# Attention packs and channel mixer on one core: another order of the opening's 939 words

## The chip, the cores and the metric

One core of a Trainium2 chip runs the whole program. The metric is the device time of one execution in microseconds (us); the time before is the median of three runs, 764.49 us (764.2 to 765.55).

## The reference, cut to what matters

```python
def sm_attn(qq, kk, vv):
    s = scale * np.matmul(qq, kk.transpose(0, 1, 3, 2))
    a = np.exp(s - np.max(s, axis=-1, keepdims=True))
    return np.matmul(a / (np.sum(a, axis=-1, keepdims=True) + 1e-09), vv)

# q, k, v: 8 batches, 8 heads, 576 rows, 64 columns; p: 32 packs for each head
p_packed = sm_attn(p, k, v)                # phase 1
out = sm_attn(q, p_packed, p_packed)       # attention of a batch
x = out.transpose(0, 2, 1, 3).reshape(8, 576, 512)
h = x.transpose(0, 2, 1) @ U @ V           # mix along the rows, rank 32
u = x + h.transpose(0, 2, 1)
return u + np.maximum(u @ w_ch1, 0) @ w_ch2    # 512 -> 2048 -> 512
```

U, V, w_ch1 and w_ch2 come as 64-bit floats and are converted on the chip.

## The kernel before, in words

Phase 1 packs the attention of p over k and v for all 8 batches. Its unit is four heads of one batch, so there are 16 units. For each the kernel loads k (`lk`) and v (`lv`, three DMAs), turns k in three pieces on TensorE (PE; `k0`, `k1`, `k2`) and copies each piece out of PSUM into `kT` (`k0a`, `k1a`, `k2a`, lines 310 and 312), multiplies with p (`s0`, line 321), takes the row maximum on VectorE (DVE; `s1`) and the exponential on ScalarE (ACT; `s2`), turns the result back (`b0`, `b1`, lines 327 and 329), copies that into `eT` (`b0a`, `b1a`, lines 672 and 674), and multiplies with v (`m0`, line 696, 40 matmuls: "the unit's product"). `m1` scales the product, `m2` keeps it, `h0` (line 709) turns it, `h1` (line 715) copies it and `h2` stores it for later.

The first batch is worked in between. The weights arrive as 512 KB blocks of bits (`w0` for w_ch1, `z0` for w_ch2) in a ring of two buffers (four for some early ones). A block is converted in a serial chain: one step on ACT (`w1`, `z1`, line 79), three on DVE (`w2` to `w4`, `z2` to `z4`, lines 80 to 82); w_ch2 is then split into a high part on ACT (`z5`, line 214) and a low part on DVE (`z6`, line 218), since matmuls here run as three products of high and low parts. `q0` to `q2` with their copies, `s3` to `sa`, `t0` to `t3`, `x0` to `x2` and `y0` to `y3` are the attention and the row mix of batches 0 and 1. `f0` folds packs into w_ch1 (line 562; `f1`, `f2` split it), `g0` is half a block of the first product of the channel mixer (six matmuls, lines 100 to 102), `e0`, `e1` and `l0` its high part, its last rows and its low part, `G0` a tile of the second product, `ad` the residual.

One string, `opening`, writes the order of all this by hand: 939 words. The program walks through it and calls, for every word, the next stage of that name (`lk` the next unit's k load, and so on). Nothing is reordered after that: each engine, and SP's queue of DMAs, works its own instructions in the order in which the words issue them, and waits where another engine's result or a free buffer is missing. A word that ends in an extra `v` puts a copy on DVE; without it the copy is ACT's. This choice exists for 116 copies: the `k?a`, `b?a` and `q?a` words, `p1` and `h1`. SP's queue holds the loads and stores: `lk`, `lp`, `lv`, `w0`, `z0`, `u0`, `v0`, `a0`, `h2`, `pu`, `ge`.

PSUM tiles come in pairs of banks by tag: `k` for the turns of k and for `g0`; `t` for p0, the heads, the folds and all of the attention; `m` for b0, b1 and m0 until `G0` starts. A word takes a free bank of its pair when it is issued. k has three buffers in SBUF, v three, and one bank pair `s` serves `s0` alone. Behind the opening a loop over the blocks of the second batch begins, and then strings of words for batches 2 to 7; these don't change. Its first step issues two halves of the first product and then the last four tiles (kt = 15) of the first batch's second product, which need the last block of w_ch2.

Of the kernel before, what the change touches and what calls it, by code (L numbers as in the profile page):

```python
# [20 lines left out]
def packed_attention_mixer_kernel(  # L21
# [49 lines left out]
    U, V, w1, w2 = (a.bitcast(I32) for a in (U, V, w1, w2))  # L71
# [83 lines left out]
    def bits_tile():  # L155
        return pipe.tile([P, 512, 2], I32, name="bits", bufs=2)

    opening = (
# [28 lines left out]
    )  # L187
    NW1 = 8

# [1153 lines left out]
    for b in late:  # L1343
        s0, s1 = sweeps[b]
# [94 lines left out]
```

## Time and profile before

| | before |
|---|---|
| median of three runs | 764.49 us |
| the profiled execution | 765.2 us, its span 763.2 |
| PE, PE's weight loads | 749.9 us (98%), 662.2 us (87%) |
| DVE, ACT, POOL | 587.5 (77%), 405.7 (53%), 84.9 us (11%) |
| DMA | 151.78 MB, mean 199 GB/s |
| granted TensorE clock | 1.0 throughout |

The span runs from the first to the last instruction; the execution's own time lies 2.0 us above it. PE's busy time counts each matmul from its start to its modelled end, and these overlap. A window gives, for one stretch, busy time of each engine and the share of the 16 DMA engines. A chain of waits is followed back from the last instruction: each piece was released by the one before it. "Landing" is the time from the issue of a DMA to the arrival of its last byte.

### The profile page before, as it was taken

How to read it: one execution, taken by the hardware profiler on the slowest of the kernel's cores; microseconds unless marked ns; L12 is line 12 of the kernel's file. 1: busy time of each engine (PE TensorE's matmuls, PEld its weight loads, DVE VectorE, ACT ScalarE, POOL GpSimd, SP SyncE). 2: the span in 40 equal slices, each digit the busy share in tenths (PEclk: the TensorE clock that was granted, in tenths of full speed). 3: DMA queues.
4: the chain of work that ended last, by engine and by line, in shares of the span. 5: the costliest groups of instructions: out<-in, count | busy, mean ns of one | idle time of the engine just before them, and what ended most of it. 6: DMA issues, size and time to landing. Idle time of an engine off the chain costs nothing.

```text
span 763.2 us, 19553 instructions
## 1 busy us (share of the span) xinstructions
PE 749.9 (98%) x7795; PEld 662.2 (87%) x7795; DVE 587.5 (77%) x1216; ACT 405.7 (53%) x1018; POOL 84.9 (11%) x116
## 2 busy tenths in 40 slices
PE   8999999999999999999999999999999999999997
PEld 6667787887878889998999989999999989999997
DVE  4799789976787768867888768867887678764876
ACT  4788765554343645555455544555554554555451
POOL 1123111010111002100201002010201020200000
PEclk9999999999999999999999999999999999999999
DMA  9999984369112874656478474657464746463672
GB/s 318 337 355 305 324 219 157 112 228 300 40 42 88 254 250 140 221 195 200 130 229 267 132 245 148 185 168 244 145 192 166 253 126 202 148 239 125 198 224 105
DMA packets 106090, 151.78 MB, mean 199 GB/s; under 512 B 40464, under 2 KB 60176, under 8 KB 102416
## 3 DMA queue, kind: packets, MB, share of 16 engines
q1 hardware_dynamic: 105856, 150.28, 61.6%
q8 instruction: 62, 1.02, 0.5%
q14 instruction: 28, 0.23, 0.1%
q10 hardware_dynamic: 144, 0.26, 0.1%
HBM read 116.56 MB, written 33.95 MB: 197 GB/s over the span
## 4 chain that ended last, share of the span: by engine, by line
PE 85%; DMA 6%; DVE 4%; ACT 3%; issue 1%; SPq 0%; POOL 0%; ACTq 0%
PE o L1085 33%; PE h_ps L100 9%; PE h_ps L101 8%; PE h_ps L102 8%; PE t_ps L562 4%; PE o L100 3%; PE o L101 3%; PE o L102 3%; DMA w1s<-w1D 2%; DMA kx<-in_k_dram 2%; PE t_ps L301 1%; PE o L1114 1%; PE s_ps L321 1%; PE t_ps L321 1%; PE m_ps L696 1%
## 5 line engine op out<-in xcount | busy, mean ns | idle before, releaser
L1085 PE MATMUL o<-w2h,h 128*128 128x256 f32 x832 | 166.9, 281 | 0.0
L100 PE MATMUL h_ps<-ah,wth 128*128 128x256 f32 (+1 forms) x512 | 157.5, 308 | 0.6 <-ACT hj L801 0.3
L101 PE MATMUL h_ps<-al,wth 128*128 128x256 f32 (+1 forms) x512 | 150.4, 294 | 0.0
L102 PE MATMUL h_ps<-ah,wtl 128*128 128x256 f32 (+1 forms) x512 | 150.3, 294 | 0.0
L1085 PEld LDWEIGHTS o<-w2h,h 128*128 128x128 f32 x832 | 136.2, 189 | 2.6 <-issue 2.6
L1074 DVE TENSOR_TENSOR h<-bits,h 128x896 fp32r<-128x896 f32 (+1 forms) x104 | 107.8, 1037 | 31.2 <-ACT h L1069 30.5
L1069 ACT CAST h<-bits 128x896 fp32r<-128x896 f32 (+1 forms) x104 | 93.7, 901 | 58.0 <-DVE bits L1048 39.7
L100 PEld LDWEIGHTS h_ps<-ah,wth 128*128 128x128 f32 x512 | 96.4, 188 | 25.2 <-ACT ppall L1034 8.4
L1085 PE MATMUL o<-w2l,h 128*128 128x256 f32 x416 | 116.0, 279 | 0.0
L101 PEld LDWEIGHTS h_ps<-al,wth 128*128 128x128 f32 x512 | 96.3, 188 | 1.0
L102 PEld LDWEIGHTS h_ps<-ah,wtl 128*128 128x128 f32 x512 | 96.3, 188 | 0.0
L1034 ACT ACTIVATE bits<-h_ps 128x256 f32<-128x256 f32 x132 | 49.5, 385 | 67.4 <-PE h_ps L102 51.5
L1085 PE MATMUL o<-tb,h 128*128 128x256 f32 x468 | 81.2, 282 | 0.1
L1085 PEld LDWEIGHTS o<-w2l,h 128*128 128x128 f32 x416 | 78.1, 188 | 0.0
L576 DVE TENSOR_TENSOR wtl<-t_ps,wth 128x256 fp32r<-128x256 f32 x128 | 49.4, 417 | 29.4 <-ACT wth L574 28.3
L1085 PEld LDWEIGHTS o<-tb,h 128*128 128x128 f32 x468 | 66.7, 189 | 0.6 <-DVE h L1074 0.3
L1046 DVE TENSOR_TENSOR bits<-bits 128x256 f32<-128x256 f32 x96 | 42.9, 447 | 28.6 <-ACT bits L1034 28.4
L574 ACT CAST wth<-t_ps 128x256 fp32r<-128x256 f32 x128 | 42.6, 376 | 27.0 <-PE t_ps L562 20.4
L452 POOL TENSOR_TENSOR al<-aT,ah 128x320 fp32r<-128x320 f32 (+1 forms) x32 | 31.4, 985 | 207.0 <-ACT ah L448 178.4
L100 PE MATMUL o<-w2h,h 128*128 128x512 f32 x128 | 52.1, 407 | 0.0
L101 PE MATMUL o<-w2l,h 128*128 128x512 f32 x128 | 50.6, 395 | 0.0
L102 PE MATMUL o<-w2h,h 128*128 128x512 f32 x128 | 50.5, 395 | 0.0
(212 smaller groups left out, 1379.8 us busy)
## 6 DMA issues: line engine op xcount, KB each, us to landing
w1s<-w1D SPq DMA_DIRECT2D x24, 1024.0 KB, 5.5
tc<-tD SPq DMA_DIRECT2D x94, 256.0 KB, 3.1
bits<-in_moe_w_ch_dram SPq DMA_DIRECT2D x32, 512.0 KB, 4.6
kx<-in_k_dram SPq DMA_DIRECT2D x16, 576.0 KB, 5.9
x<-in_q_dram SPq DMA_DIRECT2D x16, 576.0 KB, 5.9
out_dram<-os SPq DMA_DIRECT2D x33, 256.0 KB, 2.9
vt<-in_v_dram SPq DMA_DIRECT2D x32, 256.0 KB, 6.1
hD<-ppall SPq DMA_DIRECT2D x30, 256.0 KB, 4.1
```

The source lines that it names most:

```text
L100: nc.tensor.matmul(ps, lhsT=lh, rhs=rh, start=start, stop=False)
L101: nc.tensor.matmul(ps, lhsT=lh, rhs=rl, start=False, stop=False)
L102: nc.tensor.matmul(ps, lhsT=ll, rhs=rh, start=False, stop=stop)
L452: nc.gpsimd.tensor_tensor(al, aT[:, ns], ah.bitcast(F32), op=ALU.subtract)
L562: nc.tensor.matmul(f_ps[g][xs], lhsT=ppT[b][zs, g, xs], rhs=w[zs, h // 2], start=True, stop=True)
L574: nc.scalar.copy(hi[:, g], src)
L576: nc.vector.tensor_tensor(lo[:, g], src, hi[:, g].bitcast(F32), op=ALU.subtract)
L1034: nc.scalar.activation(dst[:, 256 * (i % 2):256 * (i % 2) + 256], src, AF.Relu)
L1046: vec(l[:, 4:6], s[:, 1:3], s[:, 0:1].to_broadcast([P, 2, P]), op=ALU.add)
L1069: nc.scalar.copy(h[:, ks], src)
L1074: nc.vector.tensor_tensor(lo[:, ks], src, h[:, ks].bitcast(F32), op=ALU.subtract)
L1085: nc.tensor.matmul(ps, lhsT=a, rhs=b, start=x not in self.begun, stop=last and i == 2)
```

## The change

The 939 words of `opening` stand in another order; each name occurs as often as before. 45 of the 116 copies change engines: 26 go from ACT to DVE (`k0a` five, `b1a` five, `k1a` four, `h1` three, `p1`, `b0a`, `k2a` and `q2a` two each, `q0a` one), 19 from DVE to ACT (`h1` five, `k2a` four, `b0a` four, `k1a`, `p1` and `q1a` two each). ACT has 85 of them before and 78 after. The diff replaces the whole string; its first lines, the place around the last product of phase 1, and its last lines:

```diff
-        "w0 lk lp u0 lk lk lp w1 w2 k1 k2 p0 k1av v0 k2a w0 u1 k0 p1 u2 w3 k0a lk k2 u2 lp u2 s0 k2a w0 u3 lv k0 s1 "
-        "k1 k0a w4 v3 k1a k0 lk s2 k1 k0av k1a s0 u3 b0 s1 p0 b1 k2 p1 k1 s2 k2av lk b0av lp k0 v1 r0 w0 v2 b1 s0 lv "
...
-        "w4 s3 sa w0 e1 e0 ad h2 l0 s4 s4 s5 w1 l0 s6 m0 w2 g0 w3 m1 m2 G0 w4 e0 w1 g0 l0 w0 w2 G0 w3 h0 G0 w4 h1 s7 "
...
-        "e1 z1 z6 G0 z2 G0 z3 G0 e0 f2 g0 z4 l0 G0 e0 f2 f1 l0 G0 z1 z5 g0 z2 z6 G0 z3 g0 e0 f2 y2 z4 G0 y3 e0 e1 l0 "
-        "f1 G0 z5 pu G0 z6 G0 f2 l0 "
+        "lk k1 lp lp p0 p0 lk v0 k0 lk lv p1 k1av k0av k0 w0 k2 k2a lp lk k2 k2a s0 s1 k1 s2 b1 b0 k0a k0 k1av s0 b0a "
+        "k0av lk k1 v1 k2 k1a k2a s1 p0 k0 p1v u0 w0 w0 lp lk k1 k1av s2 s0 w1 b1 k1 w2 v2 v2 b1av b1av k0a s1 k1av lv "
...
+        "h0 lv h1 w2 g0 w3 w1 h0 G0 e0 G0 w4 w0 s8 h1 w2 g0 q1a w3 w4 t0 s3 r1 e0 z6 w1 s9 sa s4 ad s4 s5 m0 s6 s7 w0 "
...
+        "e1 g0 z6 G0 e0 l0 g0 G0 z1 z2 z3 z4 y2 G0 y3 y2 y2 z5 f1 e1 G0 f1 z0 z1 f2 z6 G0 f2 G0 z2 e0 e0 l0 g0 G0 l0 z3 "
+        "G0 g0 z4 e1 z5 z6 y2 G0 G0 G0 e0 z1 z2 e0 l0 l0 z3 z4 y3 z5 z6 f1 f1 f2 f2 y3 y3 G0 "
```

What stands ahead of a unit's product in the two whole strings, where the counts differ (units count from 0; loads and stores are those issued up to and with the unit's `lv`, PE words those ahead of its `m0`):

| unit | loads and stores, old to new | PE words, old to new |
|---|---|---|
| 6 | `w0` 8 to 7, `h2` 0 to 1 | `b0` 8 to 9, `h0` 6 to 5 |
| 10 | `z0` 2 to 1 | `y0` 4 to 2 |
| 11 | the same | `g0` 0 to 1, `h0` 10 to 9 |
| 12 | the same | `g0` 2 to 3 |
| 13 | `z0` 4 to 3, `h2` 3 to 2 | `h0` 13 to 11, `b1` 15 to 14 |

In the new string 12 PSUM tiles are still to be read by a later word when the second next tile of the same pair opens; in the old string there is none.

## Rows read from the trace of the kernel before

**Rows 1.** The page, part 1: busy time and share of the span.

```profile
PE 749.9 (98%) x7795; PEld 662.2 (87%) x7795; DVE 587.5 (77%) x1216; ACT 405.7 (53%) x1018; POOL 84.9 (11%) x116
```

**Rows 2.** Windows: length, busy us of PE, PEld, DVE, ACT, POOL, clock, DMA share, GB/s.

```profile
0.00:20.00 20.00, 16.74 (x182) 12.33 (x184) 9.01 (x22) 9.71 (x24) 3.01 (x14) 1.00 0.93 321
20.00:85.00 65.00, 61.66 (x1061) 43.35 (x1062) 56.90 (x115) 54.11 (x148) 14.97 (x29) 1.00 1.01 328
85.00:167.00 82.00, 81.03 (x744) 65.47 (x743) 72.20 (x145) 45.73 (x118) 11.39 (x13) 1.00 0.66 203
```

**Rows 3.** DMA issues of 20 to 85 us: count, size each, median us to landing.

```profile
kx<-in_k_dram SPq DMA_DIRECT2D x10, 576.0 KB, 6.4
bits<-in_moe_w_ch_dram SPq DMA_DIRECT2D x10, 512.0 KB, 6.3
...
ppTd<-ppTa SPq DMA_DIRECT2D x4, 128.0 KB, 5.4
```

**Rows 4.** Chain of waits, 46 to 56 us: start, length, what.

```profile
46.31 8.43 DMA vt<-in_v_dram
...
54.87 1.04 PE m_ps L696 x40
```

**Rows 5.** Waits of 0 to 167 us: total us, times, longest.

```profile
PE k_ps L301 <- DMA kx<-in_k_dram: 2.0, 2, 1.1
...
PE m_ps L696 <- DMA vt<-in_v_dram: 0.4, 1, 0.4
...
ACT os L79 <- DMA bits<-in_moe_w_ch_dram: 9.6, 9, 3.0
...
DVE os L80 <- ACT os L79: 12.5, 14, 4.7
```

**Rows 6.** Timeline of PE: unit 13's product, and the second batch's first matmul.

```profile
85.31 0.90 PE L696 MATMUL m_ps<-vt,eT 128*32 128x64 f32 x40
...
166.57 0.31 PE L100 MATMUL h_ps<-ah,wth 128*128 128x320 f32 x1
```

**Rows 7.** Chain of waits: what one word's matmuls take on PE.

```profile
24.21 0.44 PE m_ps L327 x4
...
78.07 0.15 PE h_ps L100
...
140.11 0.29 PE t_ps L441 x2
```

**Rows 8.** Groups of 0 to 167 us, copies: busy us, mean ns, idle before.

```profile
L310 ACT COPY kT<-k_ps 128x512 f32<-128x512 f32 x26 | 15.2, 588 | 3.7 <-PE k_ps L301 2.7 <-ACT two L701 0.7
...
L310 DVE COPY kT<-k_ps 128x512 f32<-128x512 f32 x6 | 4.1, 684 | 1.9 <-PE k_ps L301 1.9
...
L674 ACT COPY eT<-m_ps 64x128 f32<-64x128 f32 x13 | 3.4, 265 | 0.0
...
L674 DVE COPY eT<-m_ps 64x128 f32<-64x128 f32 x2 | 0.5, 274 | 0.0
...
L715 ACT COPY ppTa<-t_ps 128x128 f32<-128x128 f32 x8 | 2.1, 267 | 2.6 <-PE t_ps L709 2.5
...
L715 DVE COPY ppTa<-t_ps 128x128 f32<-128x128 f32 x6 | 1.7, 280 | 1.0 <-DMA ppTd<-ppTa 1.0
```

**Rows 9.** Chain of waits, the start.

```profile
0.75 0.39 SPq L196
...
1.20 5.44 DMA kx<-in_k_dram
...
6.78 0.63 PE k_ps L301 x4
...
7.63 0.59 PE t_ps L626 x8
```

**Rows 10.** Timeline of DVE and PE: the last w2 block's low part, its first use.

```profile
165.29 0.69 DVE L218 TENSOR_TENSOR w2l<-os,w2h 128x512 fp32r<-128x512 f32 x1 [0.36 <-ACT w2h L214]
...
168.16 0.39 PE L100 MATMUL o<-w2h,h 128*128 128x512 f32 x1
```

45 rows, old and new, of the table opening are left out of this document.

## The prediction

> **What bounds the kernel now.** I read the page first: TensorE's matmuls are busy 98% of the span, its weight loads 87% [rows 1]. That names one engine for the whole program, but the change lies only in the first phase and first batch, so the windows come next. The opening runs until the first matmul of the second batch at 166.57 us [rows 6], and it has two stages. From 20 to 85 us the DMA engines are full (share 1.01, 328 GB/s) while PE's weight loads fill 43 of 65 us, VectorE (DVE) 57 and ScalarE (ACT) 54. From 85 to 167 us the DMA share is 0.66, PE is busy 81.0 of 82 us and DVE 72.2 [rows 2]. So the first stage is paced by loads and the second by PE, with DVE 9.8 us from full.
>
> The waits seem to deny the first half: PE waited for k 2.0 us in all and for v 0.4 us [rows 5]. They are small because the order gives PE other work until each load is in. What shows the pace is how late loads land: 6.3 to 6.4 us after issue in that stage for k and weights [rows 3], and in the chain of waits unit 6's product (a unit is four heads of one batch) starts at 54.87 us, in the moment when its v lands, 8.43 us after issue [rows 4]. ACT, which starts every weight conversion, waited 9.6 us for weight bits, and DVE 12.5 us for ACT's first step [rows 5]. A unit's product cannot run before the bytes that stand ahead of it in SP's queue are in. That is the account to keep.
>
> **The change part by part.** No word is added or removed: same 939 words, so the same matmuls, bytes and conversions. Three things move.
>
> *The loads.* At a given unit's product, count what stands ahead of it: loads in SP's queue (through its own v) and words on PE. Both orders are listed in the section on the change. One weight load is 512 KB, 0.524 MB [rows 3]; a store of packs, 128 KB, is 0.131 MB [rows 3]; at 328 GB/s [rows 2] these are 1.6 and 0.4 us. Four transposes take 0.44 us, so one about 0.11; a 320-column half of the first product is six matmuls of 0.15, so 0.9 us, and a piece of mix2 about 0.15 [rows 7]. What a mark gains is the time of the bytes that it no longer waits for, plus the PE work done ahead of it instead of behind it:
> - unit 6: one weight load fewer, one store more, -1.2 us; a turn more (0.44) and a head less (0.11) on PE: together -1.5 us.
> - unit 10: one weight load fewer, -1.6 us; two pieces of mix2 fewer on PE, +0.3: -1.3 us.
> - unit 11: equal bytes; a half product more, a head less: -0.8 us.
> - unit 12: equal bytes; a half product more: -0.9 us.
> - unit 13: one weight load and one store fewer, -2.0 us; two heads and one small transpose fewer on PE, +0.3: -1.7 us.
>
> The mean is -1.24 us. Unit 13's product, at 85.31 us [rows 6], is the last that the load stage paces: after it PE has its own work to the end of the opening. What PE has gained there it carries on, so I take -1.7 us, with -0.8 (the least of the five) as the near end. The far end is the PE idle time of both windows to 85 us, 3.26 + 3.34 us [rows 2]: PE cannot gain more than 6.6 us there.
>
> *The start.* The first load of k moves from second to first in SP's queue. It was issued at 1.20 us instead of 0.75 and landed 5.44 us later; the first transpose began at 6.78 us [rows 9]. That is at most 0.45 us earlier, and I count it at nothing: unit 13's account is in bytes from the same start of the DMA engines, and holds it already. The far ends are -0.45 and, if the later u and first weight bits hold up their conversions, +0.4 (the issue time that the weight load takes with it).
>
> *The copies.* 26 of the 45 go from ACT to DVE, 19 the other way. By size: the 512-column ones (k0a, k1a, q0a, q1a, b0a) 12 against 8, the 64x256 ones four each way, the small b1a five to DVE, the head copies three to DVE and five back, p1 two each way. With 0.684 us on DVE and 0.588 on ACT, 0.274 and 0.265, 0.280 and 0.267 [rows 8], DVE gets 4 x 0.684 + 5 x 0.274 - 2 x 0.280 = 3.5 us more and ACT 4 x 0.588 + 5 x 0.265 - 2 x 0.267 = 3.1 us less. All lie in phase 1 and the first two q turns, nearly all before 85 us. There DVE was idle 65 - 56.9 = 8.1 us [rows 2], so I count them at nothing. If that idle time is not where the copies come, the end is +3.5 us; ACT's 3.1 us could come back if ACT's queue delays a PE operand, so -3.1 us is the other end. I take 0 because both queues still have idle time beside loads that arrive late.
>
> *PSUM tiles read late.* In the new order 12 PSUM tiles are still unread, in text order, when the second next tile of the same pair of banks is opened; in the old one none. For that while the other bank serves alone and PE must wait for its copy before it can turn again. No row shows that wait. Bounds: 0, when other PE work stands between, and one whole 512-column copy each, 12 x 0.588 = 7.1 us [rows 8]. Less than nothing is excluded, since the old order has none to lose. 11 of the 12 lie in the stage paced by loads; I take 0, nearer to what PE shows there, an idle 3.34 us in 65 [rows 2].
>
> *The second stage.* The weight loads come in nearly the same order and PE's work is the same. PE was idle 1.0 us of 82 there [rows 2], so at most -1.0; cost 0. One cover is thin. The last w2 block is finished on DVE at 165.29 + 0.69 = 165.98 us and first used by PE at 168.16 [rows 10]: 2.2 us of room. If PE comes 1.7 us earlier, 0.5 is left. What is late next, once loads are not, is this block.
>
> Sum: -1.7 us on the profiled execution's 765.2 us (span 763.2, 2.0 around it): 763.5. That execution is 0.7 us above the median of the runs, 764.49; on the median the forecast is 762.8 us.
>
> One page states a rate that would give another result. The loads of the first stage ran at 328 GB/s [rows 2]. The Trainium skill, "DMA: Bandwidth & Descriptors", section "Where 436 GB/s comes from", says that for transfers between HBM and SBUF the HBM side binds at about 358 GB/s per core. The trace lies 8% below. By that rule the 65 us of 20 to 85 could be an estimated 59.6 us, 5.4 us less, if the old order and not the engines kept the rate down.
>
> **The rivals.**
> - *A faster load stream.* The new order spaces weight loads differently, and the stage runs at a higher rate than 328 GB/s. For it: landings of 6 us, with several loads sharing the engines [rows 3]. Against it: a DMA share of 1.01 leaves no idle engine to win. It ends where PE's idle time to 85 us is gone but for the wait for the first load: 6.6 less about 1.7 us at the start, -4.9, so 759.6 us.
> - *Given back at the end of the opening.* PE leaves phase 1 earlier, and the last w2 blocks, converted by the same serial chain of ACT and DVE steps behind the same two buffers of bits, are not earlier. In the new order the last z2 to z6 stand close to the end of the text, with ACT's e0 and two low parts among them. If they come 1.2 us later than before against the 2.2 us of room [rows 10], 1.0 of the 1.7 us is kept, at 2.9 us later nothing: 763.8 to 764.5 us, no change that can be told. That the words are not what sets the engines' order would end here too, but the rows speak against it: k1 and, but for k2, next p0 of the old text stand on PE in that order [rows 9].
> - *DVE becomes the bound (slower).* The place is 20 to 85 us, the price the 3.5 us of copies moved there. DVE would be busy 56.9 + 3.5 = 60.4 of 65 us. It decides if more than half of the old 8.1 us of idle time is forced (waits for ACT's first conversion step, which come from late bits [rows 5]): then the copies queue before reductions and splits that PE waits for. With all 3.5 us on the path and the 1.7 us gained: +1.8, 766.3 us.
>
> **How the numbers follow.** Forecast (762.8) 0.38; faster stream (759.6) 0.07; given back (764.2) 0.31; DVE (766.3) 0.24. Runs of this kernel can tell about 0.2%, 1.5 us, from no change. The first two are faster by more: 0.45; the third within: 0.31; the fourth slower: 0.24. The range goes from 759.6, the far end of the faster stream, to 767.3, DVE's case with 1.0 us of the banks' 7.1 on top. The forecast's own range is 761.5 to 763.7, from -3.0 to -0.8 us.
>
> **What would show it.** The first transpose before 6.7 us and unit 13's product at 83 to 84 us would show the account of bytes right, with 328 GB/s or near it in the stage. The opening's end at 164.5 to 165.2 us would show that the gain is carried. A product of unit 13 at 85 us or later, with DVE over 60 of 65 us busy, speaks for DVE; PE waiting on a copy into kT or eT for more than 0.3 us several times, for the banks; unit 13 early but the opening's end, or the first use of the last w2 block, at its old time, for the rival of the end. If the load rate or PE's work between 85 us and the opening's end changed by over 1 us, the prediction would be wrong in its ground, whatever the time.

## The result and the profile after

The changed kernel runs at 776.55 us (median of six runs, 774.89 to 780.05) against 765.19 us (764.2 to 767.57) for the kernel before beside it: the ratio is 1.0147, interval 1.0119 to 1.0175. It is 11 us slower where 1.7 us less was forecast, and outside the range. The profiled execution took 774.89 us, its span 773.0.

The page's first part shows the same work as in [rows 1]: the same 7795 matmuls, and engine times within 0.4% for PE and DVE, 0.6% for ACT and 1.1% for POOL.

```profile
PE 752.8 (97%) x7795; PEld 662.2 (86%) x7795; DVE 589.1 (76%) x1223; ACT 403.2 (52%) x1011; POOL 84.0 (11%) x116
```

So the time went into waiting, not into more work. The windows of [rows 2], of after:

```profile
0.00:20.00 20.00, 16.32 (x154) 12.03 (x154) 8.08 (x17) 7.92 (x17) 1.80 (x13) 1.00 0.92 312
20.00:85.00 65.00, 58.34 (x1020) 39.66 (x1018) 52.77 (x115) 48.90 (x134) 15.12 (x28) 0.97 0.95 304
85.00:167.00 82.00, 78.04 (x767) 62.16 (x768) 70.28 (x141) 44.33 (x115) 9.49 (x13) 1.00 0.63 192
```

In each of the three every busy number fell, but for POOL in the second: TensorE (PE) is idle 6.7 us instead of 3.3 in 20 to 85 us and 4.0 instead of 1.0 in 85 to 167; DVE and ACT do less per window too, and the loads run slower. No engine took the place of another as the bound. The landings of [rows 3] did not lengthen:

```profile
kx<-in_k_dram SPq DMA_DIRECT2D x10, 576.0 KB, 6.3
bits<-in_moe_w_ch_dram SPq DMA_DIRECT2D x10, 512.0 KB, 6.0
...
ppTd<-ppTa SPq DMA_DIRECT2D x2, 128.0 KB, 3.9
```

The marks in the timeline of PE: the first transpose of k (6.78 us before, [rows 9]), unit 13's product and the second batch's first matmul (85.31 and 166.57, [rows 6]):

```profile
5.44 0.60 PE L300 MATMUL k_ps<-ident,kx 128*128 128x128 f32 x4
...
90.17 0.90 PE L695 MATMUL m_ps<-vt,eT 128*32 128x64 f32 x40
...
176.76 0.31 PE L100 MATMUL h_ps<-ah,wth 128*128 128x320 f32 x1
```

PE starts 1.3 us earlier, is 4.9 us late at unit 13 and 10.2 us late at the end of the opening; what follows takes 596.2 us, 596.6 before. Marks of single executions are not exact: three kernels below with the old words up to unit 13 (e7, e8, e13) reach its product at 85.43 to 85.78 us, and e13, with the old words throughout, ends the opening at 167.58. (Line numbers are one lower than before from line 187 on.) The waits of PE, 0 to 167 us, which answer to [rows 5]; columns: total us, times, longest:

```profile
PE m_ps L326 <- ACT eT L673: 2.0, 1, 2.0
PE o L832 <- issue: 1.9, 1, 1.9
PE m_ps L328 <- ACT e L659: 1.2, 1, 1.2
PE s_ps L320 <- ACT e L659: 1.1, 1, 1.1
...
PE k_ps L303 <- DVE kT L309: 0.8, 1, 0.8
...
PE k_ps L303 <- DMA kx<-in_k_dram: 0.4, 1, 0.4
```

Before, PE waited longest for loads (k 2.0 us in two waits). Now the longest waits are for ACT: a copy into `eT`, an exponential. For the second one, within `ad`, the profile names no releaser. DVE's waits over 0 to 170 us turned round in the same way. In [rows 5] its longest, 12.5 us, was for ACT's first conversion step, and lower down in that view of before stood the row maximum; then the two of after:

```profile
DVE sm L655 <- PE s_ps L321: 0.6, 2, 0.4
```

```profile
DVE sm L654 <- PE s_ps L320: 9.0, 8, 2.1
...
DVE os L80 <- ACT os L79: 2.2, 6, 0.9
```

DVE used to wait for the first step of weight conversions. Now it stands with the row maximum (`s1`) at the head of its queue until PE has made the scores, and PE then waits, 1.2 us at unit 0 (L328), until DVE and ACT are through. The first stage's largest stall, in the timeline of PE, and the windows around it:

```profile
38.20 0.60 PE L300 MATMUL k_ps<-ident,kx 128*128 128x128 f32 x4
40.85 0.66 PE L326 MATMUL m_ps<-ident,e 128*128 128x128 f32 x4 [2.05 <-ACT eT L673]
```

```profile
40.00:42.00 2.00, 1.15 (x11) 1.15 (x12) 1.67 (x6) 1.84 (x5) 0.00 (x0) 1.00 1.00 334
42.00:44.00 2.00, 2.00 (x12) 1.93 (x10) 1.67 (x4) 0.72 (x2) 0.00 (x0) 0.50 1.17 313
44.00:46.00 2.00, 2.00 (x23) 0.74 (x22) 0.31 (x1) 1.19 (x4) 0.24 (x1) 0.65 1.09 288
```

PE waits 2.05 us, and behind the wait the granted clock (third number from the end) is 0.50, the lower of TensorE's two levels, and then 0.65, a window that is partly at it. That takes another 2 x (0.50 + 0.35) = 1.7 us. Before, the clock is 1.0 in every such window of the opening. But the loss does not need it: one of the six executions of the changed kernel was granted 1.0 over its span and took 775.95 us, 1.1 more than the profiled one, which had 0.997.

Added up: I took for each word the time from its first matmul to the next word's, less what that word takes in the trace of before (lower quartile over words of its kind). The rest is PE's loss: 15.1 us in the opening before, 26.6 after, 11.5 more; and 10.2 us of lag plus the 1.3 us of earlier start are 11.5. Single losses over 0.35 us are 11 with 5.7 us together before, 23 with 18.6 us after.

### The profile page after: what moved, and what is told of

It is laid out like the page before. It is cut to its first block, busy times and chain, and to the rows that moved or that the text cites. A ratio compares the mean times of both kernels' runs of the same rounds, so it can differ in the third digit from the quotient of the medians.

```text
span 773.0 us, 19566 instructions
## 1 busy us (share of the span) xinstructions
PE 752.8 (97%) x7795; PEld 662.2 (86%) x7795; DVE 589.1 (76%) x1223; ACT 403.2 (52%) x1011; POOL 84.0 (11%) x116
## 4 chain that ended last, share of the span: by engine, by line
PE 86%; DVE 3%; DMA 3%; ACT 2%; issue 1%; SPq 0%; ACTq 0%
PE o L1084 34%; PE h_ps L100 9%; PE h_ps L102 8%; PE h_ps L101 8%; PE t_ps L561 4%; PE o L100 4%; PE o L101 4%; PE o L102 4%; PE t_ps L300 2%; PE t_ps L320 1%; PE o L1113 1%; PE t_ps L418 1%; PE t_ps L326 1%; DMA kx<-in_k_dram 1%; DMA bits<-in_moe_w_ch_dram 1%
## 5 line engine op out<-in xcount | busy, mean ns | idle before, releaser
L100 PEld LDWEIGHTS h_ps<-ah,wth 128*128 128x128 f32 x512 | 96.6, 189 | 24.4 <-ACT ppall L1033 10.1
```

The lines of the kernel that those rows point to most:

```text
L100: nc.tensor.matmul(ps, lhsT=lh, rhs=rh, start=start, stop=False)
```

## Experiments

Each time stands beside runs of the kernel before on the same chip: medians 765.76 us for e1 to e4, 766.03 for e5 to e8, 766.99 for e9 to e12, 766.08 for e13 to e16.

**Copies or order.** e1: the old order, each of the 116 copies on the engine that the new string gives it. e2: the new order with the old string's engines.

```diff
 e1
-"w0 lk lp u0 lk lk lp w1 w2 k1 k2 p0 k1av v0 k2a w0 u1 k0 p1 u2 w3 k0a lk ..."
+"w0 lk lp u0 lk lk lp w1 w2 k1 k2 p0 k1av v0 k2a w0 u1 k0 p1 u2 w3 k0av lk ..."
```

> The order of before, with the changed kernel's choice of engine for its 45 copies. Three theories divide the changed kernel's 11 us among them. Engines: DVE has 3.5 us more to do in a stage where it was nearly full, so most of the loss is here, 771 to 776 us. Order: the copies cost little in a queue that was not laid out for them, 764 to 767 us. Loads (SP's queue blocked by a store): 764 to 766 us.

> The changed order, with every copy on the engine that it had before. Engines: the loss goes with the copies, 765 to 769 us. Order: the loss stays whole, 774 to 778 us, perhaps more, since this order was laid out for the other choice. Loads: it stays, 774 to 778 us, and the DMA engines still fall to about 190 GB/s between 50 and 60 us.

e1 767.89 us, ratio 1.0027 (1.0011 to 1.0043); e2 783.31 us, 1.0231 (1.0197 to 1.0266). The order alone costs 17.5 us, the engines alone 2.1; in the new order its own choice of engines gives back some 6 us (17.5 less 11.4, each over the kernel before beside it). Both came out nearest to the theory of the order, and above the ranges that it had. Busy times of 20 to 85 us in e2's trace:

```profile
20.00:85.00 65.00, 54.87 (x952) 36.38 (x952) 52.01 (x108) 46.03 (x126) 11.38 (x25) 1.00 0.90 287
```

DVE has 52.0 us of work there, less than before, in the slowest kernel but one, and 52.8 in the changed kernel. With e1's 2.1 us, DVE as the bound falls.

**SP's queue alone.** e3: the new order on all engines, SP's loads and stores in the old order up to unit 14's v. e4: the changed kernel, its first store of packs (which SP issued at 50.83 us, after 3.4 us without an issue) behind v of unit 7.

```diff
 e4, SP's words only
-... lk lp h2 lv w0 lv lk ...
+... lk lp lv w0 lv h2 lk ...
```

> The changed kernel's order on PE, ACT, DVE and POOL, but SP's queue in the order of before up to the load of v for unit 14, and in the changed order behind it. Loads: the DMA engines stay full from 10 to 85 us, unit 13's product comes at 85 to 86 us instead of 90.2, and 4 to 5 us of the 11 come back: 771 to 773 us. Order: PE's waits between 36 and 52 us stand behind copies, not loads, so unit 13's product stays at 89 to 91 us and the time at 775 to 778 us.

> The changed kernel with one word moved: the first store of packs (h2) stands in SP's queue behind the load of v for unit 7 instead of ahead of that for unit 6. Loads: the gap in which SP issued nothing (47.5 to 50.8 us) is gone, the v load of unit 6 is issued at 47 instead of 51.2 us, and 3 to 4 us come back, 772 to 774 us. Order: the v of unit 6 comes earlier but PE is late by itself at that time, so at most 1 us, 775 to 777 us. Engines: the same, 775 to 777 us.

e3 796.35 us, 1.0403 (1.0358 to 1.0448); e4 776.58 us, 1.0136 (1.0107 to 1.0166). The old load order under the new words is worst of all, which neither theory had: 30.6 us, of which half clock takes 13.7 in the profiled execution. The new words lose more with the old loads than with their own. e4 did to the loads what it should; first after, then e4:

```profile
50.00:60.00 10.00, 9.28 (x169) 6.60 (x168) 7.77 (x15) 9.19 (x24) 2.85 (x5) 1.00 0.67 189
```

```profile
50.00:60.00 10.00, 9.30 (x180) 6.46 (x177) 7.16 (x17) 8.60 (x25) 2.17 (x5) 1.00 0.97 312
```

312 GB/s for 189, PE's busy time the same, and no gain in the time. (This execution had also lost 3 us before 20 us, so its later marks are not compared.)

**Where.** The two strings can be spliced: the first n words of one, then those that are left in the other's order.

```diff
 e5: new[:164] + old's rest      e6: new[:508] + old's rest
 e7: old[:508] + new's rest      e8: old[:694] + new's rest
```

> The first 164 words of the new order (up to the copies of unit 4's turns, some 30 us), then the words that are left in the old order. Theory 'each stage loses its own time, and the losses add': in the changed kernel unit 3's product came 2.7 us late, so about 2.5 us over the kernel before, 768.3 us. Rival 'loads give it back' (the first stage is paced by loads; a PE that is late early catches up when old words follow): 765.8 us, no change. Rival 'one early loss sets off all': 774 us or more.

> The first 508 words of the new order (to just ahead of unit 13's product), then the old order's rest. Theory 'each stage loses its own time': unit 13's product 4.9 us late as in the changed kernel and that carried, about 770.7 us. Rival 'loads give it back': 766 us. Rival 'one early loss sets off all' (the second stage's stalls are what a late first stage brings): 775 to 776 us.

> The first 508 words of the old order, then the new order's rest. Theory 'each stage loses its own time': unit 13's product at its old time, the opening's end 5.3 us late (10.2 less 4.9), about 771 us. Rival 'loads give it back' (all of the loss belongs to the second stage): 775 to 776 us. Rival 'one early loss sets off all': 766 us.

> The first 694 words of the old order (to unit 15's product), then the new order's rest. Theory 'each stage loses its own time': in the changed kernel the lag grows from 8.8 us at unit 15's product to 10.2 us at the opening's end, so 1.4 us, about 767.2 us; with e7 this places the second stage's loss ahead of unit 15. Rival 'the end of the string loses it' (last weight blocks late against 2.2 us of room): 770 us or more.

| | median us | ratio (interval) | over before, us |
|---|---|---|---|
| e5, first 164 words new | 770.08 | 1.0054 (1.0040 to 1.0067) | 4.1 |
| e6, first 508 words new | 774.37 | 1.0107 (1.0090 to 1.0124) | 8.3 |
| e7, from word 509 new | 770.81 | 1.0069 (1.0056 to 1.0081) | 4.8 |
| e8, from word 695 new | 768.81 | 1.0036 (1.0022 to 1.0049) | 2.8 |

Every stretch loses by itself: 4.1, 4.2, 2.0 and 2.8 us by differences. Nothing is caught up when old words follow, and no early loss sets off the rest. The sizes are rougher than that: my theory had 2.5, 4.9, 5.3 and 1.4 us over before, and only e7 came out so. 8.3 and 4.8 make 13.1 for the 11 of the whole, since a splice costs something itself: e6's trace keeps up with that of after to unit 12's product (86.84 us for 86.55), and is 2.2 us behind it at unit 13's (92.36 for 90.17), where the splice is. The same stall comes back wherever its piece of text stands, 0.82 us for the low part of a w2 block in after and in e8, with an old beginning:

```profile
169.73 0.50 PE L101 MATMUL o<-w2l,h 128*128 128x512 f32 x1 [0.82 <-DVE w2l L217]
```

```profile
163.74 0.50 PE L101 MATMUL o<-w2l,h 128*128 128x512 f32 x1 [0.82 <-DVE w2l L217]
```

**Repairs.** e9 moves the readers of the 12 PSUM tiles forward, e10 nine words of the first stage apart, e11 five of the second; e12 makes all 26 moves.

```diff
 e9 (two of 12)
-... m0 s0 b0av k2 k2a w0 ... b1a lk w1 w2 b0 ... m1 (unit 3)
+... m0 s0 b0av k2 k2a m1 w0 ... b1a lk w1 w2 b0 ...
-... k2 ... k1 ... k0 ... k2a (unit 6)
+... k2 ... k1 k2a ... k0 ...
 e10 (unit 0's turns)
-... s2 b1 b0 k0a k0 k1av s0 b0a ...
+... s2 k0a k0 k1av s0 b1 b0 b0a ...
 e11 (one of five)
-... z5 f1 e1 G0 f1 z0 z1 f2 z6 G0
+... z5 f1 e1 z6 G0 f1 z0 z1 f2 G0
```

> The changed kernel with 12 words moved forward and nothing else: each of the 12 PSUM tiles that were read late is now read ahead of the second next tile of its pair. The changed kernel runs at about 776.5 us, 11 over the kernel before. Theory 'banks read late' as the prediction's term left at 0 (bounds 0 to 7.1): all of the first stage's 5 to 8 us comes back, 769 us. Theory 'words too close, of several kinds': only the stalls that these tiles make go, the 2.2 and 0.7 us ahead of unit 5's turns at 37.8 and 40.8 us and some tenths near 9 us, so 773 us. Rival 'loads pace the stage': 776 us.

> The changed kernel with 9 words of the first stage moved so that TensorE has other words between a unit's scores and the first turn of its exponentials (unit 0), between units 3 and 4's scores, between p's and k's turns at the start, and around units 8, 9 and 12; the late PSUM reads stay. Theory 'words too close': of the stalls at 9.3, 12.2, 19.8, 24.3, 63.5, 64.2 and 78.9 us (together 6.4 us) over half goes, 772 us. Rival 'banks read late': 776 us. Rival 'loads pace the stage': 776 us.

> The changed kernel with 5 words of the second stage moved: m1 of unit 13 two ACT steps earlier, two tiles of the second product ahead of unit 14's product, the split of a w2 block (z6) ahead of two others on DVE, one z4 behind two f2. Theory 'words too close': the stalls at 93.7, 124.8, 157.0 and 170.3 us (1.1, 1.65, 0.7, 1.2, together 4.7 us) mostly go, 772.5 us. Rival 'DVE and ACT are late as engines, not by these neighbours': the stalls move on to the next words, 776 us.

> The changed kernel with the 26 moves of the three other kernels together. Theory 'words too close, each place for itself': the gains add, 3.5 and 4.5 and 4 us, about 764.5 us, level with the kernel before. Rival 'something else paces' (loads, DVE): what one place gives back the next wait takes, 771 us or more.

e9 776.99 us, 1.0142 (1.0120 to 1.0164); e10 778.43, 1.0149 (1.0124 to 1.0174); e11 777.76, 1.0146 (1.0121 to 1.0172); e12 776.77, 1.0133 (1.0113 to 1.0153). None differs from the changed kernel. All four expectations of my theory failed. In e12 the 2.05 us wait at 40.85 is gone, and single losses over 0.35 us still make 18.5 us, in 28 places instead of 23. Its largest waits of PE and two windows:

```profile
PE s_ps L320 <- ACT e L659: 3.0, 4, 1.0
PE o L832 <- issue: 1.5, 1, 1.5
```

```profile
62.00:64.00 2.00, 1.06 (x8) 0.80 (x8) 0.94 (x4) 0.86 (x4) 0.00 (x0) 1.00 1.02 370
64.00:66.00 2.00, 1.87 (x19) 0.85 (x20) 1.33 (x5) 1.71 (x6) 0.93 (x1) 0.55 1.13 332
...
126.00:128.00 2.00, 2.00 (x24) 1.16 (x27) 0.59 (x2) 0.79 (x2) 0.55 (x1) 0.50 0.10 29
```

The waits went to other words, and two spells of half clock came for one; two other executions of e12 were granted 1.0 and took 775.12 and 776.77 us, so the loss is there without half clock too. At 62 to 64 us PE, DVE and ACT are each busy about half the time: they wait for each other. That left open what paces the first stage: loads after all, or these queues.

**Loads or queues.** e13 (old order) and e14 (new order): ten weight loads of the first stage read half of their bytes (`m`) and leave out the other half. The line for w_ch2; that for w_ch1 is changed alike, and the blocks lie in four fixed buffers:

```diff
-        nc.sync.dma_start(out=b.rearrange("p x t -> p (x t)"), in_=w2[kt * P:(kt + 1) * P, :])
+        nc.sync.dma_start(out=b.rearrange("p x t -> p (x t)")[:, :m], in_=w2[kt * P:(kt + 1) * P, :m])
```

> The kernel before, with ten weight loads of the first stage (w_ch1 blocks 4 to 8, w_ch2 blocks 0 to 4) reading only half of their bytes into buffers that stay; the other half of those blocks keeps old data, so the output is not the reference's. 2.6 MB less, 8 us of the load stream at 328 GB/s. Theory 'loads pace the first stage' (the prediction's ground): TensorE regains most of its idle time of 20 to 85 us, 3 us, 763 us. Rival 'the engines' queues pace it' (TensorE, VectorE and ScalarE wait for each other in the order of the words): no change, 766 us.

> The changed kernel with the same ten loads halved. Theory 'loads pace the first stage': in the changed kernel each load from 57 us on is used as it lands, 5 to 7 us behind the kernel before; with 8 us less of loads the 4.9 us of lag at unit 13's product go, 771 us or less. Rival 'the engines' queues pace it': loads are late because their buffers come free late, no change or under 1 us, 776 us.

e13 765.89 us, ratio 0.9997 (0.9985 to 1.0010); e14 775.50 us, 1.0121 (1.0100 to 1.0142), where the changed kernel has 1.0147. 2.6 MB less, no change in the old order, none that can be told in the new one. e13's window (before: 61.66 us busy, 1.01, 328), its wait for k (before: 2.0 us) and unit 13's product (before: 85.31):

```profile
20.00:85.00 65.00, 61.99 (x1065) 42.94 (x1059) 56.36 (x114) 53.48 (x146) 14.55 (x29) 1.00 0.92 287
```

```profile
PE k_ps L315 <- DMA kx<-in_k_dram: 0.4, 1, 0.4
```

```profile
85.78 0.90 PE L710 MATMUL m_ps<-vt,eT 128*32 128x64 f32 x40
```

(Lines stand 14 further down in e13 and e14.) Of the 2.0 us of before 0.8 are the first load at the start, and there the 0.4 of e13 lie too; the 1.1 us inside the stage are gone. Yet PE's idle time went only from 3.3 to 3.0 us: the next thing in line took the place. Unit 6's product, which had started when its v landed, came at 53.92 us for 54.87, unit 7's at 60.76 for 60.48. Nine of the ten halved loads stand ahead of unit 13's product, some 7 us at 328 GB/s, and it did not come earlier. In e14's trace the largest wait is the one of after, to the tenth:

```profile
PE m_ps L340 <- ACT eT L687: 2.0, 1, 2.0
```

**The new order's nearness in the old order.** e15 brings three pairs of dependent words together.

```diff
 e15
-... k1a k0 lk s2 k1 k0av k1a s0 u3 b0 s1 p0 b1 ...
+... k1a lk s2 b1 b0 k0 k1 k0av k1a s0 u3 s1 p0 ...
-... s0(3) ... b0 s1 p0 k1av s2 lk m0 k2av w0 b0a p1v lp s0(4)
+... s0(3) ... b0 s1 k1av s2 lk k2av w0 b0a s0(4) m0 p0 lp p1v
-... k0 k1a s8 h0 s2(8) m0 w3 h1 q0a s0(9)
+... k0 k1a s2(8) s0(9) s8 h0 m0 w3 h1 q0a
```

> The kernel before with three pairs of dependent words brought as close as in the new order: unit 0's turns of the exponentials 0.9 us of TensorE work behind its scores (2.5 before), unit 4's scores 1.5 us behind unit 3's (2.9), unit 9's 1.3 us behind unit 8's (2.2). Theory 'the engines' queues pace it': three stalls of 0.6 to 1.0 us that stay, 768.4 us, 770 with one spell of half clock. Rival 'loads pace the first stage': TensorE waits for loads a little less afterwards, 766 us.

770.04 us, 1.0050 (1.0030 to 1.0070): 4 us for three local moves. The stalls in its timeline of PE:

```profile
12.99 0.30 PE L328 MATMUL m_ps<-ident,e 128*64 128x128 f32 x1 [1.46 <-ACT e L659]
...
27.41 0.77 PE L320 MATMUL s_ps<-kT,pT 64*32 64x320 f32 x16 [1.58 <-DVE kT L311]
...
32.60 0.33 PE L708 MATMUL t_ps<-ident,two 128*128 128x128 f32 x1 [1.03 <-DVE vs L286]
...
52.48 0.77 PE L320 MATMUL s_ps<-kT,pT 64*32 64x320 f32 x16 [0.87 <-ACT e L659]
```

They sum to 4.9 us (that at 32.60 is a consequence, not one of the three), and the clock stayed up in this execution's opening. Up to the opening's end nothing absorbed them (166.57 before):

```profile
171.25 0.31 PE L100 MATMUL h_ps<-ah,wth 128*128 128x320 f32 x1
```

(The rest of this execution was 1.9 us shorter than that of before, so its time, 767.96 us, is the lowest of the six.) So in the old order dependent words that stand closer cost time, and PE has no slack behind loads to hide it.

**k first.** e16 keeps of the new order only its start: the first load of k is earlier, the first weight block and its conversion are later.

```diff
-        "w0 lk lp u0 lk lk lp w1 w2 k1 k2 p0 k1av v0 k2a w0 u1 k0 p1 u2 w3 k0a ..."
+        "lk lp lk u0 w0 lk lp k1 k2 p0 k1av v0 k2a w0 u1 k0 p1 u2 k0a ... s2 w1 w2 w3 w4 ..."
```

> The kernel before with one idea of the new order alone: the first k load at the head of SP's queue, the first weight block behind k of unit 1, its four conversion steps behind the exponential of unit 0. The first transpose comes 1.4 us earlier in the changed kernel (5.4 for 6.8 us). Theory 'the engines' queues pace it': TensorE starts earlier and carries that on, up to 1.4 us, 764.6 us. Rival 'loads pace the first stage': the bytes are the same, 766 us.

767.08 us, 1.0014 (1.0001 to 1.0026). No gain. The chain of waits at e16's start (start, length, what):

```profile
2.93 5.26 DMA x<-in_moe_U_dram
...
8.30 0.35 ACT os L79
8.65 0.27 ACT pT L631
8.92 0.48 ACT kT L309
...
9.45 0.77 PE s_ps L320 x12
```

The scores stand where they stood before (9.48 us in the chain whose start is [rows 9]): ACT's copies wait in its queue behind a conversion whose load lands at 8.2 us.

## Why the prediction was wrong

**The ground: "the first stage [is] paced by loads and the second by PE".** This step failed, and with it the account by bytes. The DMA share of 1.01 and loads that land just ahead of use looked like a bound. e13 takes 8 us of that stream away and nothing moves. What the runs show in its place is that the order itself sets the time, 17.5 us with the engines of before (e2), through waits of PE, DVE and ACT for each other. My reading, argued and not shown, is that the old order is balanced: loads, PE and the copies on ACT and DVE each come when the next needs them, and PE's remaining 3.3 us are waits of several kinds, of which k's is one. That unit 6's product starts in the moment when its v lands [rows 4] I read as cause; in e13 it came 1.0 us earlier, and that was lost again by unit 7. The Trainium skill, "Perfetto Trace Analysis", section "Identifying the Most-Contended Engine", says that for DMA the occupancy of the 16 engines misleads and the use of HBM is to be read instead. On the first half the trace agrees: share 1.01 in the old order, 0.92 in e13, one time. The second half would not have helped here, since the rate also fell, from 328 to 287 GB/s, at one time.

**The units' gains (-0.8 to -1.7 us).** All five signs were wrong: +3.4 us at unit 6, then +4.3, +5.4, +5.8, and +4.9 at unit 13. The counts at these five units are right, but the section on the change says that they are the units where the counts differ, and that is not so: they differ at the others as well (ahead of unit 4 the new order has a k load and a weight load more and a p load fewer, ahead of unit 7 one fewer of each of the three). By e13 the bytes ahead do not decide.

**The start (0, at most -0.45).** The first transpose came 1.3 us earlier, three times the bound, because the load also took less time (it landed at 4.8 us, 4.0 behind its issue, for 5.44). As forecast nothing of it arrived: e16 +1.0 us, and in the changed kernel the first scores start at 9.6 us for 9.5.

**The copies (0, bounds -3.1 to 3.5).** 2.1 us in the old order (e1), inside the bounds; in the new order a gain of some 6 us, outside them. So the same choice of engines cost time in one order and gained it in the other, and busy time does not tell its worth. That it depends on whose queue is blocked at each word is my reading.

**PSUM tiles read late (0, bounds 0 to 7.1).** The wait that "no row shows" is there: 2.05 us at 40.85. The sign named for it, waits of over 0.3 us on copies into kT or eT, came as well. But e9, without any late reader, is no faster, so the sign did not tell the banks from other waits. As a term of a sum it is neither 0 nor 2; another wait stands behind it. (10 of the 12 late readers lie ahead of unit 13's product, not 11.)

**The second stage (0, "at most -1.0").** e7 measures 4.8 us. I had bounded only what could be gained from 1.0 us of idle time. With PE nearly full a new wait is nearly all loss, and busy times gave that no upper bound. Of the rival "given back at the end" the place was right (the low parts of w2 blocks, 0.82 us; e8 2.8 us in the last stretch), but there was no gain to give back. Its sum was off as well: by the room of 2.2 us, 1.2 us later leaves 1.0 of the 1.7, which is 763.5 and not 763.8, and nothing is left at 2.2 us later, not 2.9. The -3.0 us at the far end of the forecast's own range follows from none of the terms.

**What could have been counted** stands in both strings: how much other PE work lies between a unit's scores (`s0`) and the first turn of its exponentials, with each word's time from the trace of before. Between the two run the reduction on DVE and the exponential on ACT. In the chain of waits of before (start, length, what), unit 0:

```profile
9.48 0.77 PE s_ps L321 x12
...
11.94 0.74 ACT e L660 x2
...
13.49 0.59 PE m_ps L327 x4
```

The scores end at 10.25 us and the exponential at 12.68, so 2.4 us want other work. The old order has that at every unit but one (unit 1, 2.3; the new one 2.9 there), the new one lacks it twice, has about half as much at units 2, 4, 6 and 10, and more than the old one at 1, 5, 13, 14 and 15:

| unit | 0 | 2 | 3 | 4 | 6 | 10 | 11 |
|---|---|---|---|---|---|---|---|
| old, us | 2.5 | 5.5 | 4.4 | 8.4 | 6.2 | 9.2 | 10.1 |
| new, us | 0.5 | 2.7 | 1.8 | 4.7 | 3.3 | 4.1 | 7.9 |

That nearness costs time is shown by e15. That all of the 11 us comes from it is not, and this count names little of it: in after one wait of PE stands at a turn behind its exponential, the 1.2 us of unit 0, and none of 0.3 us or more at unit 3. The other waits stand at other pairs: scores behind the exponential ahead of them, turns behind copies, products behind splits. Nor is e12 a full test of the count: it brings unit 0 from 0.5 to 1.6 us and leaves units 2, 3, 6, 10 and 11 as they are. So what makes up the 11 us, pair by pair, and what would bring the new order level, short of the old one, stays open. Half clock is 1.7 us for each spell, one in the profiled execution of after.

None of the kernels is faster than the one before.

## What to carry to other kernels

Full DMA engines and data that is used as it lands don't prove that loads set the pace; halve the bytes of a few loads, and look whether the time moves. Where engines work in a written order, look for each dependent pair at how much other work lies between, on every queue that the pair crosses: here a stall stayed where PE had no slack (e15), and busy times gave no upper bound for it. Mending single places need not help: 26 moves, made for late readers and for stalls, gave nothing back that could be told (e12). A bound made from idle time holds for gains only.

## What the runs showed of the hardware

Half clock came in most profiled executions with new words: 1.7 us lost in each of after, e2, e5, e6, e7 and e10, 3.4 us in e9, e11, e12 and e14, 5.1 us in e4, 13.7 us in e3 (0.50 from 10 to 22 us, behind 2 us without a matmul); none in the opening of before, e1, e8, e13, e15 and e16. In after it stands right behind PE's wait of 2.05 us, in e12 behind the half idle 62 to 64 us; in e15 none came behind waits of 1.46 and 1.58 us. In after the wait and the half clock behind it make 3.7 us together.

One of DVE's conversion steps is slowed beside POOL. The timeline of after, one instruction of each:

```profile
118.94 1.16 POOL L370 TENSOR_TENSOR e<-e,s 128x576 f32<-128x576 f32 x1 [3.23 <-DVE s L382]
119.04 1.35 DVE L80 TENSOR_SCALAR os<-os 128x512 int32<-128x512 int32 x1 [0.27 <-ACT os L79]
...
164.59 0.43 DVE L80 TENSOR_SCALAR os<-os 128x512 int32<-128x512 int32 x1
```

The same step takes 0.43 us alone and 1.35 when it starts 0.1 us behind POOL's, ending 0.3 us after it. The Trainium skill, "SBUF — State Buffer", section "Who interferes with whom", says that a tensor_scalar can run in a mode that takes the port pair which VectorE shares with GpSimd, and that of the two whoever issues first keeps it for the whole instruction while the other blocks. On the blocking the trace agrees: the step ends just behind POOL's. This happens in the old order too (1.34 us at 118.08), so it does not explain the change.
